# Scores two units ahead, one layer-1 buffer, and another ScalarE order in a hand-ordered cycle

## The chip, the cores and the metric

The kernel runs on one core of a Trainium2 chip. Its time is the device time of one launch, in microseconds (us), as the median of several runs. In the profile PE is TensorE (PEld its weight loads), DVE is VectorE, ACT is ScalarE, POOL is GpSimd, and SP is the engine that here only issues DMAs. A q behind an engine's name (ACTq, SPq) is its sequencer, for instance where it issues a DMA.

## What is computed

Three layers, all in fp32. The first is attention over 4 batches, 8 heads, 576 tokens and head size 64, in which each query keeps only its 32 largest scores. The other two are feed-forward layers over 2304 tokens, 512 wide with 2048 hidden channels: layer 1 with a rational function between its two products, layer 2 with h cos(h). Cut to what matters, the reference is:

```python
scores = scale * np.matmul(q, k.transpose(0, 1, 3, 2))
kth = np.partition(scores, -top_k, axis=-1)[..., -top_k:-top_k + 1]
scores = np.where(scores >= kth, scores, -1000000000.0)
attn = softmax(scores)
x = (attn @ v), heads side by side
h = x @ w_in1
P = a[0] + a[1] * h + a[2] * h**2 + a[3] * h**3
Q = 1.0 + np.abs(b[0]) * np.abs(h) + np.abs(b[1]) * h**2
x = (P / (Q + 1e-06)) @ w_out1
h = x @ w_in2
out = (h * np.cos(h)) @ w_out2
```

## The kernel before

**Units.** The work is cut into 72 attention units, numbered i: 128 queries for a pair of heads each. Eight units make one block of 256 tokens, and each of the feed-forward layers has eight groups (256 hidden channels) for a block. Group i-9 of layer 1 and group i-18 of layer 2 run beside unit i (UA = 9, UB = 18 line 39), so that each step of the outer loop holds a bit of all three layers. Units 64 to 71 are mixed: their queries come from two batches, so each loads two k tiles and two v tiles and has more, smaller matmuls.

**Attention.** `qk(i)` (line 313) makes the scores of a unit for two heads. TensorE multiplies q, split into a high and a low part, with k, four matmuls for each head, and ScalarE copies each head's scores out of PSUM into a tile sS (line 319, two buffers). `topk(i)` (line 341) runs on VectorE. It takes the elementwise max and min of the two halves of the scores (`tensor_tensor`), finds the 32nd largest by rounds of `max` and `match_replace` in a tile e, then ScalarE makes Exp into e, and in the last step, which is issued in the next unit, VectorE masks and sums (`scalar_tensor_tensor`). `av(i)` (line 390) transposes e on TensorE (pp), ScalarE copies the transposes (pt), and TensorE multiplies with v. q comes by DMA (`load_q`, line 179, tile qr); `high_q` (line 186) rounds it to the high part on ScalarE, and `low_q` subtracts. k comes by `load_k` (line 196, two buffers, shared by the two units of a pair), v by `load_v`. `prep` and `store_k` (lines 172 and 162) split the k of later batches and store both parts.

**Layer 1.** `in1` and `in1b` (two halves of h on TensorE), `copy1` (line 501: w = h and r = |h| on ScalarE), `lin1` (q and u on ScalarE), `pol1` (q and u multiplied on GpSimd), `rec1` (Ln and Exp into r on ScalarE), `mid1` and `end1` (lines 524 and 528: four passes on VectorE, then ScalarE copies the result's high part into gg), `low1` (its low part, GpSimd), `out1` (24 matmuls into y). The tiles w, q and r have N1 = 2 buffers, u has NU = 2.

**Layer 2.** `in2` and `in2b`, `phase2` (line 577: ScalarE copies h to hs, then makes rr and n from it), `mid2` (VectorE), `sin2` (one Sin on ScalarE over two groups, in even units: the sine units; it needs a table load), `table` (loads the table of Exp and Ln again), `mul2` (GpSimd), `high2` (ScalarE copies the high part into gg), `low2` (GpSimd), `out2` (12 matmuls into o). In each unit h of layer 1, h of layer 2 and the two pp share two PSUM buffers.

**Order.** Up to unit 19 and from step 72 on, a planner places the instructions (`free`, line 724, and `events`, line 774, give the order that it starts from). From unit 20 to 71 (U0 and U1), the fixed cycle, `unit(i, prev)` (line 806) writes the order out by hand: class `InOrder` ties each instruction of VectorE, ScalarE, GpSimd and TensorE to the one written before it on its engine. GpSimd's instructions also wait for the last VectorE instruction written before them that is not `max` or `match_replace`. DMAs of q, k and v are issued from ScalarE's queue, so they stand in its order too; weights come by SP, through four stream buffers. Four lines of `unit` carry most of what follows:

```python
            nq = qk(i + 1) if i + 1 < nu else iter(())
            ev(i - UB - 2, high2)
            ev(i - UB, phase2)
            high_q(i + 3)
```

`qk(i + 1)` stands between the halves of h, `high2` ahead of Exp, `phase2` and `high_q` at the end of ScalarE's unit, just ahead of the next unit's pt copies. What the diff touches, and what calls it:

Of the kernel before, what the change touches and what calls it, by code (L numbers as in the profile page):

```python
# [51 lines left out]
PM = 150  # L52
WA, PA = 12, 90
WG, PG = 10, 90
N1, NU, N2, NST, NGG = 2, 2, 2, 4, 3
SUBV = (3,)
CPE = (0, 2)
LAL = 3
DV1, DV2 = 8, 7
KB, VB, XB = 2, 2, 2  # L60
OBB, EB = 1, 2
QRB, QB = 2, 2
S0 = 46
U0, U1 = 20, 72
# [51 lines left out]
def body(tc, out, qt, kt, vt, ident_d, w1_d, w1o_d, a_d, b_d, w2_d, w2o_d):  # L116
# [5 lines left out]
    with ExitStack() as ctx:  # L122
# [60 lines left out]
                A.dma_start(out=raw, in_=qt[k, pr, :, :, i % 2 * P:(i % 2 + 1) * P])  # L183
                qs_[i] = [raw, None]

        def high_q(i):
            if 8 <= i < nu:
                qs_[i][1] = x = att.tile([P, 2, 2, P], F32R, tag="q", bufs=QB, name=f"q{i}")
                A.activation(x[:, 0], qs_[i][0], AF.Copy)

        def low_q(i, E):
            if 8 <= i < nu:
# [120 lines left out]
        def qk(i):  # L313
            n, pr = units[i]
            raw, x = qs_.pop(i)
            hi, lo = (x[:, 0], x[:, 1]) if x is not None else (None, None)
            kvs = ins[i]
            m = P // len(kvs)
            st[i] = sb = att.tile([P, 2, S], F32, tag="sS", bufs=2, name=f"sS{i}")
            for j in range(2):  # L320
                rows = slice(j * D, (j + 1) * D)
                for c, (k, _) in reversed(list(enumerate(kvs))):
                    qs = slice(0, (c + 1) * m)
                    for hf in range(2):
                        o = sx[qs, hf, :HALF]
                        hs = slice(hf * HALF, (hf + 1) * HALF)
                        if n < 2:
                            mm = PE.matmul(o, raw[rows, j, qs], k[rows, 0, hs].bitcast(F32), start=True, stop=True)
                            after(mm, hf)
                        else:  # L330
                            mm = PE.matmul(o, hi[:, j, qs], k[:, j, hs], start=True, stop=False, skip_group_check=True)
                            after(mm, hf)
                            mm = PE.matmul(o, lo[:, j, qs], k[:, j, hs], start=False, stop=True, skip_group_check=True)
                        order[hf] = [mm.ins.name]
                A.activation(halves(sb[:, j]), sx[:, :, :HALF], AF.Copy)
                if j == 0:
                    yield
            if n == 1:
                store_k(kvs[0][0], 0, pr)
# [234 lines left out]
        def in2b(k, g):  # L574
            g2[k, g][1](1)

        def phase2(k, g):
            h, _ = g2.pop((k, g))
            if g % SINB == 0:
                rp[k, g // SINB] = late[0].tile([P, SINB, 512], F32, tag="rr", bufs=2, name=f"rr{k}_{g}")  # L580
            rs = rp[k, g // SINB]
            rr = rs[:, g % SINB]
            hs = late[0].tile([P, 512], F32, tag="hs", bufs=N2, name=f"hs{k}_{g}")
            A.activation(hs, h, AF.Copy)
            n = late[0].tile([P, DM], F32, tag="n", bufs=OBB, name=f"n{k}_{g}")
            if k >= DV2:
                V.tensor_scalar(rr, hs, 1.0 / TWO_PI, 0.25, op0=ALU.mult, op1=ALU.add)
            else:
                A.activation(rr, hs, AF.Identity, scale=1.0 / TWO_PI, bias=quarter)
            A.activation(n, rr, AF.Identity, bias=magic)  # L590
            rt[k, g] = rr, hs, n
# [125 lines left out]
        preps = {}  # L717
        for b in range(1, B):
            for pr in range(NP):
                preps.setdefault(16 * b - PL + pr if b == 1 else 16 * b - PL + 1 + 2 * pr, []).append((b, pr))  # L720

        nrm, low, held, x2, ob = [], [], [], [], []

        def free(i, prev):
            nq = qk(i + 1) if i + 1 < nu else iter(())
            next(nq, None)
            next(nq, None)
            if i + 2 < nu:
                load_k(i + 2)
            t = topk(i) if i < nu else iter([None] * 9)  # L730
            fresh = []
            for p in range(5):
                if p == 0:
                    for x, a in held:
                        store_k(x, *a)
                    held[:] = [(prep(*a), a) for a in preps.get(i, [])]
                    if prev is not None:
                        next(prev)
                    next(t, None)
                    if prev is not None:  # L740
                        next(prev)
                    next(t, None)
                    if prev is not None:
                        a = av(i - 1)
                        next(a)
                        next(a, None)
                        if i % 4 == 0:
                            nrm.append(norm((i - 1) // 8, (i - 1) // 4 % 2))
                            next(nrm[-1])
                            next(nrm[-1])  # L750
                            fresh.append(nrm[-1])
                    if 0 < i < nu:
                        load_v(i)
                    low_q(i + 2, G)
                else:
                    next(t, None)
                if p == 1:
                    if i + 1 < 8:
                        load_q(i + 3)
                    if i + 2 >= 8:  # L760
                        load_q(i + 4)
                if p == 2:
                    high_q(i + 3)
                if fresh and p == 1:
                    next(fresh.pop())
                if len(nrm) == 2 and p in (1, 4):
                    for x in nrm[:1] if p == 1 else nrm[1:]:
                        next(x)
                        next(x, None)
                    if p == 4:  # L770
                        nrm.clear()
                yield t

        def events(u, p):
# [16 lines left out]
            if p == 2:  # L791
                if u < U0:
                    ev(u - UA - 1, end1, low1)
                ev(u - UB, in2, in2b, phase2)
            if p == 3:
                ev(u - UA - 1, out1)
                if last(u - UA - 1):
# [6 lines left out]
                    store((u - UB - 3) // NG, 1)  # L804

        def unit(i, prev):
            t = topk(i)
            next(t)
            next(prev)
            next(prev)  # L810
            a = av(i - 1)
            next(a)
            ev(i - UA - 1, mid1, end1)
            for x in low:
                next(x, None)
# [18 lines left out]
            ev(i - UB - 2, mul2)  # L834
            if i % 4 == 0:
                next(nrm[-1])
            ev(i - UA, in1b, copy1)
            nq = qk(i + 1) if i + 1 < nu else iter(())
            next(nq, None)
            ev(i - UA, lin1, pol1)  # L840
            ev(i - UB, in2)
# [2 lines left out]
            for k in ob:  # L844
                store(k, 1)
            ob.clear()
            if i + 2 < nu:
                load_k(i + 2)
            load_q(i + 4)
            load_v(i)  # L850
            ev(i - UA - 1, out1)
            ev(i - UB - 3, out2)
            ev(i - UB - 1, table)
            ev(i - UB - 2, high2)
            for _ in range(4):
                next(t)
            ev(i - UA, rec1)
            if i % 8 == 0:
                for x in nrm:
                    next(x)  # L860
                low.extend(nrm)
                nrm.clear()
            ev(i - UB, phase2)
            high_q(i + 3)
            if last(i - UA - 1):
                x2high((i - UA - 1) // NG)
                x2.append((i - UA - 1) // NG)
# [70 lines left out]
```

## Time and profile before

| | |
|---|---|
| three runs | 1452.74 us median (1451.27 to 1456.11) |
| the profiled execution's own time | 1454.12 us |
| its span, first to last instruction | 1452.3 us |
| busy in the span | PE 88%, PEld 77%, DVE 83%, ACT 76%, POOL 40% |
| mean granted TensorE clock | 0.922 |
| chain of work that ended last, by engine | PE 45%, ACT 20%, DMA 3%, issue 3%, DVE 2% |

The busy shares are means over stages that differ: a head with weight conversion and a cold clock, the fixed cycle, and a tail without attention. A unit of the fixed cycle is told by VectorE's max/min pair (`e<-sS`, TENSOR_TENSOR), which starts it; the pair of unit 22 starts at 402.3 us, that of unit 64 at 1109.6. The granted clock is a share of 2.4 GHz: 1.00 is that level, 0.5 is 1.2 GHz, and what lies between is a stretch with some of each. Almost all instructions are recorded under one helper's line (L80), so groups go by the tiles' names, out<-in.

### The profile page before, as it was taken

How to read it: one execution, taken by the hardware profiler on the slowest of the kernel's cores; microseconds unless marked ns; L12 is line 12 of the kernel's file. 1: busy time of each engine (PE TensorE's matmuls, PEld its weight loads, DVE VectorE, ACT ScalarE, POOL GpSimd, SP SyncE). 2: the span in 40 equal slices, each digit the busy share in tenths (PEclk: the TensorE clock that was granted, in tenths of full speed). 3: DMA queues.
4: the chain of work that ended last, by engine and by line, in shares of the span. 5: the costliest groups of instructions: out<-in, count | busy, mean ns of one | idle time of the engine just before them, and what ended most of it. 6: DMA issues, size and time to landing. Idle time of an engine off the chain costs nothing.

```text
span 1452.3 us, 25010 instructions
## 1 busy us (share of the span) xinstructions
PE 1272.2 (88%) x8944; PEld 1121.2 (77%) x8944; DVE 1200.8 (83%) x2514; ACT 1100.5 (76%) x1918; POOL 585.1 (40%) x434
## 2 busy tenths in 40 slices
PE   6777776667799999999998999999999899999988
PEld 3434555556788888888888888888888788899976
DVE  7989997898888988889899889989998778755532
ACT  7777887866688887878888778878887667777642
POOL 3666455633344444444444443534444324430000
PEclk9567797878899999999999999999999999999999
DMA  8986777862366676556677755655666667667667
GB/s 267 333 273 208 222 228 252 292 202 80 102 204 206 214 230 212 190 178 207 211 227 232 235 185 186 198 197 192 207 206 228 239 224 258 216 207 247 227 217 233
DMA packets 155948, 314.98 MB, mean 217 GB/s; under 512 B 12592, under 2 KB 47536, under 8 KB 155824
## 3 DMA queue, kind: packets, MB, share of 16 engines
q1 hardware_dynamic: 122832, 261.99, 54.4%
q10 hardware_dynamic: 32992, 51.39, 11.1%
q8 instruction: 71, 1.16, 0.3%
q14 instruction: 53, 0.43, 0.1%
HBM read 278.20 MB, written 35.13 MB: 216 GB/s over the span
## 4 chain that ended last, share of the span: by engine, by line
PE 45%; ACT 20%; DMA 3%; issue 3%; DVE 2%; ACTq 2%; POOL 1%; SPq 0%
PE h L80 22%; PE sx L80 9%; PE y L80 7%; PE o L80 6%; ACT r L80 4%; ACT e L80 3%; ACTq L80 2%; ACT q L80 2%; ACT rr L80 2%; DMA lo<-w2lo 1%; ACT n L80 1%; ACT gg L80 1%; DMA w2o<-w2o 1%; ACT sS L80 1%; DVE e L80 1%
## 5 line engine op out<-in xcount | busy, mean ns | idle before, releaser
L80 DVE MAX8 hd<-e 128x8 f32<-128x288 f32 (+1 forms) x576 | 320.7, 596 | 0.0
L80 DVE TENSOR_TENSOR e<-sS 128x576 f32<-128x576 f32 x144 | 172.9, 1240 | 87.1 <-ACT sS L80 74.2
L80 PE MATMUL y<-gg,w1o 128*128 128x256 f32 x1152 | 219.7, 289 | 13.3 <-DVE x2l L80 6.5
L80 DVE MATCH_REPLACE8 e<-hd,e 128x288 f32<-128x288 f32 (+1 forms) x432 | 231.0, 541 | 0.0
L80 PE MATMUL h<-xh,w1hi 128*128 128x256 f32 x576 | 183.2, 318 | 47.9 <-ACT pt24a L80 2.1
L80 PE MATMUL o<-w2o,gg 128*128 128x512 f32 x864 | 212.1, 393 | 3.6 <-DMA w2o<-w2o 3.5
L80 POOL TENSOR_TENSOR gg<-rr,gg 128x512 fp32r<-128x512 f32 x56 | 72.5, 1295 | 315.6 <-DVE rr L80 84.1
L80 PEld LDWEIGHTS y<-gg,w1o 128*128 128x128 f32 x1152 | 184.9, 196 | 16.6 <-ACT gg L80 11.5
L80 PEld LDWEIGHTS o<-w2o,gg 128*128 128x128 f32 x864 | 157.5, 189 | 35.0 <-DMA w2o<-w2o 4.7
L80 PE MATMUL h<-xh,lo 128*128 128x256 f32 x576 | 171.4, 298 | 0.9 <-DMA lo<-w1lo 0.9
L80 PE MATMUL h<-xl,w1hi 128*128 128x256 f32 x576 | 170.9, 297 | 0.0
L80 PEld LDWEIGHTS h<-xh,w1hi 128*128 128x128 f32 x576 | 117.7, 204 | 68.8 <-issue 7.1
L80 PE MATMUL h<-x2h,lo 128*128 128x256 f32 x576 | 164.0, 285 | 3.0 <-DMA lo<-w2lo 3.0
L80 PE MATMUL y<-gg,w1ol 128*128 128x256 f32 x576 | 165.3, 287 | 0.0
L80 PE MATMUL h<-x2h,w2hi 128*128 128x256 f32 x576 | 163.5, 284 | 0.5 <-ACT hs L80 0.5
L80 PE MATMUL h<-x2l,w2hi 128*128 128x256 f32 x576 | 163.6, 284 | 0.1
L80 DVE SCALAR_TENSOR_TENSOR e<-sS,hd,e 128x576 f32<-128x576 f32 x144 | 123.1, 883 | 39.3 <-ACT e L80 39.3
L80 POOL TENSOR_TENSOR q<-q,r 128x512 f32<-128x512 f32 x64 | 86.2, 1347 | 133.3 <-ACT q L80 133.3
L80 POOL TENSOR_TENSOR cb<-cb,raw 128x512 int32<-128x512 int32 x64 | 92.8, 1454 | 73.2 <-DVE cb L80 59.6
L80 PEld LDWEIGHTS h<-xh,lo 128*128 128x128 f32 x576 | 118.5, 206 | 1.4 <-DMA lo<-w1lo 1.4
L80 PEld LDWEIGHTS h<-xl,w1hi 128*128 128x128 f32 x576 | 118.4, 206 | 1.0 <-issue 0.7
L80 PE MATMUL sx<-k,q 128*128 128x288 f32 (+1 forms) x576 | 106.8, 313 | 11.2 <-ACT xs L80 9.1
(1023 smaller groups left out, 3343.0 us busy)
## 6 DMA issues: line engine op xcount, KB each, us to landing
w2o<-w2o SPq DMA_DIRECT2D x144, 512.0 KB, 4.4
lo<-w1lo SPq DMA_DIRECT2D x72, 512.0 KB, 4.6
w1ol<-w1ol SPq DMA_DIRECT2D x72, 512.0 KB, 4.9
lo<-w2lo SPq DMA_DIRECT2D x72, 512.0 KB, 4.2
k<-kdr ACTq DMA_DIRECT2D x44, 576.0 KB, 3.9
raw<-w SPq DMA_DIRECT2D x32, 512.0 KB, 4.9
v<-vt ACTq DMA_DIRECT2D x48, 320.0 KB, 6.2
qr<-qt ACTq DMA_DIRECT2D x72, 128.0 KB, 3.9
```

The lines of the kernel that those rows point to most:

```text
L80: r = f(*a, **k)
```

## The change

The scores of unit i+2, not i+1, are made in unit i of the fixed cycle; sS gets a third buffer, an extra `qk` at the end of unit 19 starts the lead, and `load_k` and `prep` shift by one unit with it. w, q and r of layer 1 get one buffer instead of two. q's high part is a GpSimd copy within the cycle, between `mul2` and `pol1`. `phase2` is cut in two: `copy2` (hs) stays in its unit, the rest runs at the end of units without the sine, and early in the next unit for a group whose own unit has the sine. `high2` moves behind `rec1` and `copy2`, `load_q` up behind `copy1`, `load_v` down behind Exp.

```diff
@@ -52,13 +52,13 @@
 PM = 150
 WA, PA = 12, 90
 WG, PG = 10, 90
-N1, NU, N2, NST, NGG = 2, 2, 2, 4, 3
+N1, NU, N2, NST, NGG = 1, 2, 2, 4, 3
 SUBV = (3,)
 CPE = (0, 2)
 LAL = 3
 DV1, DV2 = 8, 7
 KB, VB, XB = 2, 2, 2
-OBB, EB = 1, 2
+OBB, EB, SB = 1, 2, 3
 QRB, QB = 2, 2
 S0 = 46
 U0, U1 = 20, 72
@@ -183,10 +183,13 @@
                 A.dma_start(out=raw, in_=qt[k, pr, :, :, i % 2 * P:(i % 2 + 1) * P])
                 qs_[i] = [raw, None]
 
-        def high_q(i):
+        def high_q(i, grouped=False):
             if 8 <= i < nu:
                 qs_[i][1] = x = att.tile([P, 2, 2, P], F32R, tag="q", bufs=QB, name=f"q{i}")
-                A.activation(x[:, 0], qs_[i][0], AF.Copy)
+                if grouped:
+                    G.tensor_copy(x[:, 0], qs_[i][0])
+                else:
+                    A.activation(x[:, 0], qs_[i][0], AF.Copy)
 
         def low_q(i, E):
             if 8 <= i < nu:
@@ -316,7 +319,7 @@
             hi, lo = (x[:, 0], x[:, 1]) if x is not None else (None, None)
             kvs = ins[i]
             m = P // len(kvs)
-            st[i] = sb = att.tile([P, 2, S], F32, tag="sS", bufs=2, name=f"sS{i}")
+            st[i] = sb = att.tile([P, 2, S], F32, tag="sS", bufs=SB, name=f"sS{i}")
             for j in range(2):
                 rows = slice(j * D, (j + 1) * D)
                 for c, (k, _) in reversed(list(enumerate(kvs))):
@@ -574,14 +577,17 @@
         def in2b(k, g):
             g2[k, g][1](1)
 
+        def copy2(k, g):
+            h, _ = g2.pop((k, g))
+            hs = late[0].tile([P, 512], F32, tag="hs", bufs=N2, name=f"hs{k}_{g}")
+            A.activation(hs, h, AF.Copy)
+            rt[k, g] = hs
+
         def phase2(k, g):
-            h, _ = g2.pop((k, g))
+            hs = rt[k, g]
             if g % SINB == 0:
                 rp[k, g // SINB] = late[0].tile([P, SINB, 512], F32, tag="rr", bufs=2, name=f"rr{k}_{g}")
-            rs = rp[k, g // SINB]
-            rr = rs[:, g % SINB]
-            hs = late[0].tile([P, 512], F32, tag="hs", bufs=N2, name=f"hs{k}_{g}")
-            A.activation(hs, h, AF.Copy)
+            rr = rp[k, g // SINB][:, g % SINB]
             n = late[0].tile([P, DM], F32, tag="n", bufs=OBB, name=f"n{k}_{g}")
             if k >= DV2:
                 V.tensor_scalar(rr, hs, 1.0 / TWO_PI, 0.25, op0=ALU.mult, op1=ALU.add)
@@ -717,7 +723,7 @@
         preps = {}
         for b in range(1, B):
             for pr in range(NP):
-                preps.setdefault(16 * b - PL + pr if b == 1 else 16 * b - PL + 1 + 2 * pr, []).append((b, pr))
+                preps.setdefault(16 * b - PL + pr if b == 1 else 16 * b - PL + 2 + 2 * pr, []).append((b, pr))
 
         nrm, low, held, x2, ob = [], [], [], [], []
 
@@ -769,6 +775,10 @@
                         next(x, None)
                     if p == 4:
                         nrm.clear()
+                if i == U0 - 1 and p == 4:
+                    for _ in qk(i + 2):
+                        pass
+                    load_k(i + 3)
                 yield t
 
         def events(u, p):
@@ -791,7 +801,7 @@
             if p == 2:
                 if u < U0:
                     ev(u - UA - 1, end1, low1)
-                ev(u - UB, in2, in2b, phase2)
+                ev(u - UB, in2, in2b, copy2, phase2)
             if p == 3:
                 ev(u - UA - 1, out1)
                 if last(u - UA - 1):
@@ -804,12 +814,15 @@
                     store((u - UB - 3) // NG, 1)
 
         def unit(i, prev):
+            sine = (i - UB - 1) % SINB == SINB - 1
             t = topk(i)
             next(t)
             next(prev)
             next(prev)
             a = av(i - 1)
             next(a)
+            if not sine:
+                ev(i - UB - 1, phase2)
             ev(i - UA - 1, mid1, end1)
             for x in low:
                 next(x, None)
@@ -834,8 +847,10 @@
             ev(i - UB - 2, mul2)
             if i % 4 == 0:
                 next(nrm[-1])
+            high_q(i + 3, True)
             ev(i - UA, in1b, copy1)
-            nq = qk(i + 1) if i + 1 < nu else iter(())
+            load_q(i + 4)
+            nq = qk(i + 2) if i + 2 < nu else iter(())
             next(nq, None)
             ev(i - UA, lin1, pol1)
             ev(i - UB, in2)
@@ -844,24 +859,24 @@
             for k in ob:
                 store(k, 1)
             ob.clear()
-            if i + 2 < nu:
-                load_k(i + 2)
-            load_q(i + 4)
-            load_v(i)
+            if i + 3 < nu:
+                load_k(i + 3)
             ev(i - UA - 1, out1)
             ev(i - UB - 3, out2)
             ev(i - UB - 1, table)
-            ev(i - UB - 2, high2)
             for _ in range(4):
                 next(t)
+            load_v(i)
             ev(i - UA, rec1)
             if i % 8 == 0:
                 for x in nrm:
                     next(x)
                 low.extend(nrm)
                 nrm.clear()
-            ev(i - UB, phase2)
-            high_q(i + 3)
+            ev(i - UB, copy2)
+            ev(i - UB - 2, high2)
+            if not sine or i == U1 - 1:
+                ev(i - UB, phase2)
             if last(i - UA - 1):
                 x2high((i - UA - 1) // NG)
                 x2.append((i - UA - 1) // NG)
```

## Rows read from the trace of the kernel before

**Rows 1.** Stages: us, busy of PE, PEld, DVE, ACT, POOL; PEclk, DMA share, GB/s

```profile
0.00:362.60 362.60, 257.43 (x1303) 187.97 (x1303) 319.25 (x657) 269.85 (x512) 185.90 (x140) 0.78 0.73 236
362.60:402.30 39.70, 31.95 (x235) 29.60 (x236) 31.00 (x67) 26.44 (x48) 14.62 (x11) 0.83 0.33 106
402.30:1109.60 707.30, 665.60 (x5045) 611.45 (x5044) 638.26 (x1384) 577.75 (x1003) 313.49 (x230) 0.97 0.63 207
1109.60:1262.00 152.40, 140.48 (x1164) 130.63 (x1164) 120.34 (x265) 111.87 (x191) 54.77 (x44) 0.97 0.67 235
1262.00:1452.30 190.30, 176.71 (x1204) 161.53 (x1202) 91.94 (x144) 114.57 (x167) 16.36 (x13) 0.98 0.69 227
```

**Rows 2.** The same view for units 35, 38 and 40

```profile
623.67:642.33 18.66, 16.43 (x118) 15.00 (x117) 14.69 (x33) 12.62 (x23) 5.89 (x5) 0.91 0.54 195
...
675.08:690.51 15.43, 15.29 (x121) 14.09 (x120) 14.82 (x32) 13.99 (x24) 6.94 (x6) 1.00 0.61 198
...
707.07:722.92 15.85, 15.71 (x125) 14.51 (x124) 15.06 (x35) 14.53 (x25) 8.19 (x7) 1.00 0.55 177
```

**Rows 3.** Waits, 402 to 1110 us: total us, times, longest

```profile
POOL q L80 <- ACT q L80: 105.6, 43, 5.0
...
DVE e L80 <- ACT sS L80: 47.4, 38, 2.9
...
DVE e L80 <- ACT e L80: 22.3, 21, 2.0
```

**Rows 4.** The chain that ended last, 600 to 760 us: start, us, what

```profile
632.62 2.93 PE h L80 x12
...
673.95 1.43 PE h L80 x12
...
681.01 0.45 PE pp37a L80 x4
...
703.26 0.54 PE sx L80 x4
```

**Rows 5.** PE's timeline: start, us, instruction, [idle before, what ended it]

```profile
632.62 0.58 PE L80 MATMUL h<-xh,w1hi 128*128 128x256 f32 x1 [1.53 <-ACT pt34a L80]
```

**Rows 6.** ACT's timeline, 689 to 708 us

```profile
689.85 0.63 ACT L80 ACTIVATE sS<-sx 128x576 f32<-128x576 f32 x1
...
691.07 1.28 ACT L80 ACT_TABLE_LOAD   x1 [0.59 <-issue]
...
693.12 1.45 ACT L80 ACTIVATE e<-sS,nb 128x576 f32<-128x576 f32 x2
...
696.37 0.72 ACT L80 ACTIVATE rr<-hs,quarter 128x512 f32<-128x512 f32 x1
...
697.75 0.40 ACT L80 ACTIVATE q<-qr 128x256 fp32r<-128x256 f32 x1
698.05 0.58 ACT L80 ACTIVATE pt38a<-pp38a 128x512 f32<-128x512 f32 x1
...
706.40 0.64 ACT L80 ACTIVATE sS<-sx 128x576 f32<-128x576 f32 x1
...
707.69 1.45 ACT L80 ACTIVATE e<-sS,nb 128x576 f32<-128x576 f32 x2
```

**Rows 7.** POOL's groups, 402 to 1110 us: busy us, mean ns | idle before

```profile
L80 POOL TENSOR_TENSOR u<-u,w 128x512 f32<-128x512 f32 x43 | 76.5, 1780 | 0.0
...
L80 POOL TENSOR_TENSOR gg<-rr,gg 128x512 fp32r<-128x512 f32 x42 | 54.0, 1285 | 231.0 <-DVE rr L80 61.3 <-DVE x2l L80 35.3 <-ACT pt56t L80 8.7
```

**Rows 8.** The tile e on DVE, whole span: ns min/median/max, first and last start

```profile
L80 DVE TENSOR_TENSOR e<-sS x144: 734/945/1965, 10.9 to 1245.1; 128x576 f32<-128x576 f32 x144
```

**Rows 9.** DVE's timeline, q's low part in unit 39

```profile
698.18 0.43 DVE L80 TENSOR_TENSOR q<-qr,q 128x256 fp32r<-128x256 f32 x1
```

**Rows 10.** Timelines of ACT, then DVE, at the edge of unit 20

```profile
360.57 0.80 ACT L80 ACTIVATE q<-r,babs 128x512 f32<-128x512 f32 x1
...
361.63 1.02 DVE L80 SCALAR_TENSOR_TENSOR u<-q,u 128x512 f32<-128x512 f32 x1
```

## The prediction

> **What bounds the kernel now.** I read the stages first. The fixed cycle (units 20 to 71) has three pieces: two starting units, 42 plain units from 402.3 to 1109.6 us, and eight mixed units to about 1262 [rows 1]. The 42 take 707.3 us, 16.84 us each. No engine is busy that long: TensorE 665.6 us (15.85 a unit), VectorE 638.3 (15.20), ScalarE 577.8 (13.76). TensorE's mean granted clock is 0.97, so some of its 665.6 us ran at 1.2 instead of 2.4 GHz; taking 0.03 x 707.3 = 21.2 us off leaves 644.4, or 15.34 us a unit.
>
> Single units come next. One in which nothing stalls takes 15.43 us at a clock of 1.00; one in four that also transposes the softmax sums takes 15.85; an odd one took 18.66 at 0.91 [rows 2]. So 3/4 x 15.43 + 1/4 x 15.85 = 15.54 us is what TensorE needs, and 1.30 us a unit is lost, mostly in the odd units. The waits tell on what: VectorE waits 47.4 us in these 42 units for the copy of scores (sS) and 22.3 us for Exp (e) [rows 3]. TensorE's loss shows in the chain of waits: twelve matmuls of h from 632.62 took 2.93 us [rows 4], after 1.53 us of idling for ScalarE's copy of the transposes (pt34a) [rows 5].
>
> ScalarE's timeline says why the copy was late. The second score copy (sS) of unit 38 starts at 689.85. DMA issues keep the table load until 691.07, Exp starts at 693.12, phase2's rr at 696.37, the q copy at 697.75, and pt38a only at 698.05: 8.20 us. In the next unit the piece from sS to Exp is 707.69 - 706.40 = 1.29 us, and with the same 4.93 us behind Exp that makes 6.22 [rows 6]. TensorE in the meantime has its last half of h, y and o, and the next transposes: from 673.95 to 681.01 + 0.45 = 7.51 us [rows 4]. So after one unit of two ScalarE is late by 0.7 us even if Exp never waits for VectorE, and it does wait, because VectorE only gets the scores that were made within the same unit.
>
> **The change part by part.**
> *Scores two ahead, three sS buffers.* The eight score matmuls and two copies a unit stay where they are on their engines; only their index moves. The max/min of the next unit then finds its scores a unit old. The 47.4 us of waits go [rows 3], and VectorE may run ahead. What is late next for VectorE is Exp. A new wait: qk(i+2) now needs low_q(i+2) of the same unit. VectorE made q's low part at 698.18 [rows 9] and the scores' matmuls came at 703.26 [rows 4]: 5.1 us of cover, costed at nothing; without it up to that much would go onto TensorE, with y and o queued behind. load_k runs a unit earlier and keeps its two buffers and its one-unit lead; its issue moves from sine units, where the table load waits for it, to the others. prep and its stores on SP move a unit later with it, off the unit of the k load, so no two of them fight for a buffer: nothing.
>
> *ScalarE's order.* In a sine unit the stretch from sS to pt loses the DMA issues in front of the table load (691.07 less 689.85 + 0.54 of sS = 0.68), the q copy (0.30) and rr and n of phase2 (697.75 - 696.37 = 1.38): 8.20 - 2.36 = 5.84 us. In the other it loses only q: 6.22 - 0.30 = 5.92 [rows 6]. high2's copy moves behind Exp inside that stretch and weighs the same. Both are below TensorE's 7.51 by 1.6 us, which is what VectorE may keep Exp waiting. The deferred phase2 (1.38) goes where ScalarE waits for TensorE in the next unit, which has no sine; VectorE's mid2 waits for it, at most that long, and max and match_replace queue behind; the new lead covers it. load_q is issued under the copies of w and r, load_v under Exp: nothing, if their buffers are free, as they are by a unit.
>
> *One buffer for w, q and r.* copy1 must then wait for end1 of the group before. VectorE is through with end1 when it starts q's low part (698.18) [rows 9], before the scores' matmuls (703.26) [rows 4] that follow the half of h that copy1 reads: covered. In the whole trace the second buffer is used once, at the edge of the cycle: ScalarE writes the new q at 360.57 while VectorE reads the old one until 361.63 + 1.02 = 362.65 [rows 10]. That costs 2.1 us at most; I take it whole.
>
> *q by GpSimd.* No row has a one-input copy on GpSimd. The nearest, a two-input pass over 128x512, is 1.285 us, so half of it for 256 columns, 0.64, and the dearest row, u at 1.78, bound it [rows 7]; I take 0.64, the row of the same engine without contention, scaled. GpSimd idles 105.6 us before the q product, 2.5 a unit [rows 3]: hidden at either end. Below nothing it cannot go; what ScalarE gains is counted above. In the Trainium skill, the page "GPSIMD Engine Reference", section "Engine selection", speaks against elementwise work on GpSimd but calls one-input passes roughly line-rate. No run here shows that; by it the sum stays and the slower rival below would have no chance.
>
> *The sum.* TensorE needs 15.54 us a plain unit; VectorE, if it keeps today's 22.3 / 42 = 0.53 of Exp waits, needs 15.20 + 0.53 = 15.73. I take 15.85, a little above both, for the joints between engines that no longer have slack: 42 x (16.84 - 15.85) = 41.6 us. The bounds are 15.54 (54.6) and 16.84 (0). The mixed units take 152.4 / 8 = 19.05; TensorE's need is 140.5 less 0.03 x 152.4, over 8, or 17.0 [rows 1]. I take 17.6, since each loads two k and two v and k keeps its place in ScalarE's queue: 8 x 1.45 = 11.6, between 0 and 16.4. The first two units take 39.7 with VectorE busy 31.0 [rows 1]; scores made ahead in unit 19 save about half of the 8.7: 4.3, between 0 and 8.7. Less 2.1. Together 41.6 + 11.6 + 4.3 - 2.1 = 55.4. The head (362.6 us) and the tail (190.3, TensorE busy 176.7) [rows 1] keep their order of work; I put them at 0, within 5 us either way, since they are placed by a planner that sees other buffers. The profiled execution took 1454.1 us (its span and 1.8 around it): 1398.7. It is 1.4 us above the median of the runs, so 1397.
>
> **The rivals.** *ScalarE still holds TensorE.* VectorE has only 1.6 us of ScalarE's margin. If Exp comes later than that in units without the sine, where two phases stand behind it, the transposes' copy is late in every second unit, TensorE idles and its clock falls. In rows, the same twelve matmuls cost 2.93 us after idling [rows 4], and the unit ran at 0.91 [rows 2]. For it: all three engines then need 14 to 15.7 us of 15.9. Against: VectorE's lead outlasts the late phase2. With a third of today's 1.30 recovered the plain units give 18, the mixed 6, the rest 0: about 1430. The Trainium skill, "TensorE: Matmul & The Clock Gate", section "What's actually happening", has the clock throttled by default and released by activity. The trace agrees (0.91 after idling, 1.00 without), and by that rule what is left of the stalls would keep paying double.
>
> *VectorE's max/min keeps colliding with GpSimd.* A max/min pass takes 0.73 us at least and 0.945 in the median [rows 8]; u on GpSimd, which runs beside it, takes 1.78 where the same shape takes 1.285 [rows 7]. The 15.20 holds this already, so with it VectorE is at 15.73, inside the forecast.
>
> *Slower: the copy on GpSimd.* It stands before both products of pol1, and Ln waits for q. The cover is 2.5 us a unit [rows 3]; past that each us of copy is a us of unit, and the gain of 0.99 is gone at about 3.5, plus what ScalarE's margin takes, 1.6: from some 5 us the kernel is slower. A copy of 7 would cost 2 us x 50 units: about 1550. Against: it would be four times the dearest row.
>
> *The scores come no earlier in effect.* If the k tiles, still two, made qk(i+2) wait, VectorE would get its scores as now and only ScalarE's order would help: some 10 us, 1443. Against: k is needed a unit earlier and is loaded a unit earlier.
>
> **How the numbers follow.** Forecast 0.74; ScalarE holds TensorE 0.14; scores no earlier 0.05, half of it within what can't be told from no change; GpSimd or something like it slower 0.05; no effect 0.02. A measurement of this kernel tells 0.3%, 4.4 us, from no change. Faster 0.74 + 0.14 + 0.025 rounds to 0.91, same 0.04, slower 0.05. The low end has every bound of the sum at its best but for the last us of each: 54.6 + 16.4 + 8.7 - 2.1 = 77.6, or 1375; the high end reaches past the first rival, 1432.
>
> **What would show it.** Right: plain units of 15.5 to 16.2 us in place of 15.4 and 16.5 to 19; VectorE's waits for sS gone, those for Exp left; granted clock 1.00 over the 42 units; table loads without DMA issues in front; the GpSimd copy near 0.6 us. Wrong: TensorE idle before h for pt copies in every second unit; qk waiting for q's low part or for q from GpSimd; ScalarE's w waiting for VectorE; head or tail longer by over 5 us.

## The result, and the profile after

The changed kernel takes 1387.89 us in the median of four runs (1384.79 to 1389.19), against 1452.26 for the kernel before measured with it: a ratio of 0.9549, with a 95% interval of 0.9525 to 0.9573. The profiled execution took 1387.8 us, with a span of 1386.0. The forecast was 1397, in a range of 1375 to 1432.

The stages of the span, with the columns of [rows 1], cut at the starts of units 20, 22 and 64 and behind unit 71:

```profile
0.00:361.40 361.40, 242.68 (x1290) 179.53 (x1291) 321.56 (x656) 269.03 (x512) 181.06 (x138) 0.82 0.73 237
361.40:396.10 34.70, 31.78 (x268) 29.18 (x268) 30.86 (x66) 28.61 (x50) 19.50 (x15) 1.00 0.41 134
396.10:1061.20 665.10, 652.70 (x5051) 598.65 (x5050) 625.80 (x1386) 566.82 (x962) 312.52 (x271) 1.00 0.67 221
1061.20:1194.00 132.80, 130.03 (x1119) 121.02 (x1118) 111.99 (x261) 105.73 (x178) 55.89 (x47) 1.00 0.73 254
1194.00:1386.00 192.00, 178.88 (x1225) 164.16 (x1224) 96.28 (x149) 116.72 (x172) 19.15 (x15) 0.98 0.69 228
```

The plain stretch fell from 707.3 to 665.1 us: 15.84 us a unit, with TensorE busy 652.7 of it (15.54 a unit) at a clock of 1.00. TensorE's busy time fell by 12.9 us and its idle time by 29.3. The 42 units give back 42.2 us, the starting units 5.0, units 64 to 70 17.2 (19.15 to 16.69 us a unit, by the starts of units 64 and 71: 1109.60 and 1243.65 before, 1061.17 and 1177.99 after), and head and tail together 1.8. That is the 66.3 us by which the span is shorter.

Units now come in unequal pairs, because VectorE runs ahead in one and waits in the next; a pair is the right measure. The same view for units 36 and 37, then 38 and 39:

```profile
618.00:649.67 31.67, 31.17 (x245) 28.62 (x244) 29.45 (x68) 27.58 (x48) 15.19 (x14) 1.00 0.64 216
649.67:680.94 31.27, 30.80 (x241) 28.26 (x240) 29.07 (x66) 25.59 (x44) 13.93 (x13) 1.00 0.66 212
```

The waits from 396 to 1061 us, which answer to [rows 3]:

```profile
DVE rr L80 <- ACT n L80: 37.2, 21, 2.4
POOL q L80 <- ACT q L80: 33.2, 39, 2.3
...
PEld sx L80 <- ACT sS L80: 12.6, 40, 0.6
```

VectorE's groups, with the idle time before them at the end of the line:

```profile
L80 DVE TENSOR_TENSOR e<-sS 128x576 f32<-128x576 f32 x85 | 90.0, 1098 | 0.0
L80 DVE SCALAR_TENSOR_TENSOR e<-sS,hd,e 128x576 f32<-128x576 f32 x84 | 65.0, 809 | 0.3 <-ACT e L80 0.3
```

VectorE's 47.4 us for sS are gone, and of the 22.3 for Exp 0.3 is left. In their place VectorE waits in every second unit for n of the deferred phase2, 1.8 us in the mean; none of TensorE's idle time is put down to that wait. TensorE's groups by what idled before them say where its time was lost. The line of h is the kernel's before, then that of the changed kernel, each in its own fence, with busy time, mean ns, and idle time before the group:

```profile
L80 PE MATMUL h<-xh,w1hi 128*128 128x256 f32 x336 | 106.8, 318 | 36.9 <-ACT pt24a L80 2.1 <-ACT pt40a L80 2.1 <-ACT pt42a L80 1.9
```

```profile
L80 PE MATMUL h<-xh,w1hi 128*128 128x256 f32 x336 | 103.4, 308 | 7.9 <-ACT pt25a L80 1.0 <-ACT pt41a L80 1.0 <-ACT pt57a L80 0.4
...
L80 PE MATMUL sx<-k,q 128*128 128x288 f32 (+1 forms) x352 | 65.1, 309 | 4.5 <-ACT sS L80 1.4
```

TensorE idled 36.9 us before h in the kernel before, nearly all of it for ScalarE's copies of the transposes, and 7.9 after; this is the number to follow through the experiments. Of the 7.9, 5.2 are 0.14 us in each of 37 units, which is there even where ScalarE itself waits for TensorE; 2.7 us, in units 25, 33, 41, 49 and 57, lie behind a late copy. The second line is a small new wait: 4.5 us ahead of the score matmuls.

ScalarE's timeline over a sine unit (36), to be held against [rows 6]:

```profile
629.49 0.63 ACT L80 ACTIVATE r<-w 128x512 f32<-128x512 f32 x1
629.50 0.56 ACTq L80 DMA_DIRECT2D qr<-qt  x1
630.11 0.65 ACT L80 ACTIVATE sS<-sx 128x576 f32<-128x576 f32 x1
...
632.07 0.63 ACT L80 ACTIVATE sS<-sx 128x576 f32<-128x576 f32 x1
632.72 1.28 ACT L80 ACT_TABLE_LOAD   x1
...
634.25 0.78 ACT L80 ACTIVATE e<-sS,nb 128x576 f32<-128x576 f32 x1
...
637.36 0.62 ACT L80 ACTIVATE gg<-rr 128x512 fp32r<-128x512 f32 x1
639.15 0.60 ACT L80 ACTIVATE pt36a<-pp36a 128x512 f32<-128x512 f32 x1 [1.17 <-PE pp36a L80]
```

From the second sS to the end of the last copy it is 637.98 - 632.07 = 5.91 us, where 8.20 stood before and 5.84 was forecast, and then ScalarE waits 1.17 us for TensorE. The roles are turned round. From the second sS to the start of the pt copy it is 639.15 - 632.07 = 7.08 us; this is the time that TensorE leaves ScalarE, which the prediction had put at 7.51.

### The profile page after: what moved, and what is told of

Same layout as the page of the kernel before. It is cut to its first block, busy times and chain, and to the rows that moved or that the text cites. A ratio compares the mean times of both kernels' runs of the same rounds, so it can differ in the third digit from the quotient of the medians.

```text
span 1386.0 us, 25042 instructions
## 1 busy us (share of the span) xinstructions
PE 1236.1 (89%) x8944; PEld 1092.5 (79%) x8944; DVE 1186.5 (86%) x2514; ACT 1086.9 (78%) x1869; POOL 588.1 (42%) x483
## 4 chain that ended last, share of the span: by engine, by line
PE 51%; ACT 17%; DVE 15%; DMA 10%; issue 3%; POOL 2%; SPq 0%; ACTq 0%; POOLq 0%; DVEq 0%
PE h L80 19%; PE o L80 11%; PE y L80 10%; PE sx L80 8%; DVE e L80 7%; DVE hd L80 5%; ACT r L80 2%; ACT sS L80 2%; DMA lo<-w1lo 2%; DMA w2o<-w2o 2%; ACT e L80 1%; ACT rr L80 1%; ACT n L80 1%; DMA w2lo<-cb 1%; POOL cb L80 1%
## 5 line engine op out<-in xcount | busy, mean ns | idle before, releaser
L80 PE MATMUL y<-gg,w1o 128*128 128x256 f32 x1152 | 216.9, 287 | 9.9 <-POOL gg L80 6.9
L80 PE MATMUL h<-xh,w1hi 128*128 128x256 f32 x576 | 179.4, 312 | 11.1 <-ACT pt13a L80 1.4
L80 PE MATMUL h<-xh,lo 128*128 128x256 f32 x576 | 167.9, 291 | 1.6 <-DMA lo<-w1lo 1.6
L80 DVE TENSOR_TENSOR e<-sS 128x576 f32<-128x576 f32 x144 | 148.7, 1070 | 7.7 <-ACT sS L80 5.1
L80 DVE SCALAR_TENSOR_TENSOR e<-sS,hd,e 128x576 f32<-128x576 f32 x144 | 127.7, 914 | 15.6 <-ACT e L80 15.6
L80 ACT ACTIVATE e<-sS,nb 128x576 f32<-128x576 f32 x144 | 105.7, 770 | 19.6 <-DVE hd L80 18.5
L80 PEld LDWEIGHTS h<-xh,lo 128*128 128x128 f32 x576 | 114.7, 199 | 2.5 <-DMA lo<-w1lo 2.2
L80 PEld LDWEIGHTS h<-xl,w1hi 128*128 128x128 f32 x576 | 115.0, 200 | 2.1 <-DVE xl L80 1.2
```

The source lines that it names most:

```text
L80: r = f(*a, **k)
```

## The experiments

Two theories. Theory A, the prediction's emphasis: VectorE waited for scores, so the lead of two units is what counts. Theory B: ScalarE's copies came late and stopped TensorE; the new order is what counts, and the lead little. The table holds the whole study. A plain unit is 1/42 of the time from the start of unit 22 to that of unit 64, a mixed one 1/7 of that from 64 to 71, and the last column is the idle time of TensorE before h in the plain units, as in the fences above; these three are of one profiled execution each. That of phase_whole took 1400.1 us, 5 above its median, that of phase_loads 1401.2, 4 below.

| kernel | median us | plain unit | mixed unit | idle before h |
|---|---|---|---|---|
| before | 1452.3 | 16.84 | 19.15 | 36.9 |
| one_buffer | 1448.2 | 16.87 | 18.83 | 37.1 |
| lead_only | 1420.3 | 16.31 | 18.80 | 28.1 |
| no_lead (order only) | 1395.1 | 15.91 | 17.63 | 6.6 |
| no_lead_phase | 1401.2 | 16.06 | 17.48 | 17.5 |
| phase_loads | 1405.3 | 16.01 | 17.82 | 20.1 |
| phase_whole | 1395.4 | 15.97 | 17.06 | 13.0 |
| q_scalar | 1392.0 | 15.93 | 17.02 | 11.5 |
| high2_old | 1388.9 | 15.84 | 16.71 | 5.9 |
| loads_old | 1387.0 | 15.74 | 17.33 | 8.7 |
| changed | 1387.9 | 15.83 | 16.69 | 7.9 |
| q_five | 1400.4 | 16.13 | 16.84 | 6.3 |
| loadq_later | 1385.6 | 15.74 | 16.91 | 9.2 |
| loadq_split | 1384.4 | 15.75 | 17.01 | 9.1 |

The medians carry some 2 to 4 us either way. The head of the profiled executions, up to unit 20, ranged from 358.4 to 363.9 us among kernels that differ from the changed one only within unit(), so differences of a few us between totals are not read; the units are steadier.

### The lead and the order apart

Without the lead:

```diff
-            nq = qk(i + 2) if i + 2 < nu else iter(())
+            nq = qk(i + 1) if i + 1 < nu else iter(())
-            if i + 3 < nu:
-                load_k(i + 3)
+            if i + 2 < nu:
+                load_k(i + 2)
```

(and the extra qk at the end of unit 19 out, prep a unit earlier).

> The changed kernel with the scores of unit i+1 again made in unit i (k load and prep back with them); ScalarE's order, the one buffer and the GpSimd copy stay. Theory A (the lead is what counts, since VectorE waited for scores): VectorE waits for sS again, some 1 us a unit in the fixed cycle, and the time is 1430 to 1445. Theory B (ScalarE's late copies held TensorE, the lead only helps at the edges): within 12 us of the changed kernel, below 1400.

And the kernel before with the lead alone (with the extra qk at the end of unit 19, prep a unit later, N1 = 1 and three sS buffers, as in the changed kernel):

```diff
-            nq = qk(i + 1) if i + 1 < nu else iter(())
+            nq = qk(i + 2) if i + 2 < nu else iter(())
-            if i + 2 < nu:
-                load_k(i + 2)
+            if i + 3 < nu:
+                load_k(i + 3)
```

> The kernel before with the scores two ahead, three sS buffers, one buffer for w, q, r, and the k load and prep that go with them; ScalarE's order and its q copy stay as before. Theory A: only the sine units stay late, by ScalarE's 8.20 against TensorE's 7.51 us, 0.7 us in two units or 15.9 us a unit: 1395 to 1410, with VectorE's waits for sS gone. Theory B: ScalarE's late copies still stop TensorE and its clock falls: 1430 to 1450, granted clock below 0.99 in the plain units.

Measured: 1395.14 us without the lead (ratio 0.959, 0.9564 to 0.9616), 1420.3 with the lead alone (0.9776, 0.9752 to 0.98). Theory A fails on the first; the second lies between the two forecasts. The run without the lead brings 57 of the 64 us: the order, with q's copy on GpSimd and the one buffer, which is worth 4 us by itself (below). TensorE before h, and then VectorE's wait for scores among the waits of the plain units, in the run without the lead:

```profile
L80 PE MATMUL h<-xh,w1hi 128*128 128x256 f32 x336 | 103.5, 308 | 6.6 <-ACT pt40a L80 0.5 <-ACT pt24a L80 0.5
```

```profile
DVE e L80 <- ACT sS L80: 4.6, 14, 1.3
```

VectorE's wait for scores went from 47.4 to 4.6 us although the scores are made in the same unit as before. So that wait was a symptom. The traces fit the reading that scores came late because TensorE had stood still for the transposes' copies: in the kernels without the lead TensorE's idle time before h and VectorE's wait for scores fall together, 36.9 and 47.4 us, 17.5 and 12.3 (no_lead_phase), 6.6 and 4.6. In the first of them the clock was 0.97 besides, in the other two 1.00. With the lead alone, VectorE does not wait for scores at all, but TensorE's line and the plain stretch read:

```profile
L80 PE MATMUL h<-xh,w1hi 128*128 128x256 f32 x336 | 103.8, 309 | 28.1 <-ACT pt32a L80 1.5 <-ACT pt48a L80 1.5 <-ACT pt24a L80 1.5
```

```profile
395.30:1080.20 684.90, 655.71 (x5069) 601.49 (x5068) 659.60 (x1385) 581.79 (x1008) 310.17 (x229) 1.00 0.64 216
```

The clock is at 1.00 here too, so theory B's forecast of a clock under 0.99 missed, and so did its time, which this run undercuts by 10 us; the copies are still late. Nor does this run leave ScalarE's work in the sine units as it was: the issue of k's load, and in eight of them prep's copy of k (0.67 us), move to the other units with the lead. The two parts overlap. In a plain unit, the lead is worth 16.87 - 16.31 = 0.56 us with the old order (against one_buffer) and 15.91 - 15.83 = 0.08 with the new; the order 0.96 without the lead and 0.48 with it. In a mixed unit they do more together than apart: from one_buffer's 18.83, the lead alone brings 0.03 us, the order alone 1.20, both 2.14. Some 0.4 of what the lead brings there is only moved: with it the seven units hold 96 to 100 score matmuls, without it 112, because the scores of one mixed unit are made earlier.

### One buffer

```diff
-N1, NU, N2, NST, NGG = 2, 2, 2, 4, 3
+N1, NU, N2, NST, NGG = 1, 2, 2, 4, 3
```

> The kernel before with one buffer for w, q and r and nothing else. By the prediction it costs at most 2.1 us at the edge of unit 20 and otherwise only what the planner makes of it in the head: 1447 to 1459. Rival: in the head copy1 holds TensorE's PSUM buffer while it waits for end1, and the head grows by 10 us or more.

Measured: 1448.23 us, ratio 0.9973 (0.9956 to 0.999). Within the range, on the good side: units 20 and 21 took 33.8 us instead of 39.7, the head 366.3 instead of 362.6. The planner placed the work around the edge differently; the 2.1 us did not show as a loss. The plain units did not change (16.87).

### The order, part by part

Each of these undoes one part of ScalarE's order in the changed kernel. phase2 whole:

```diff
-            if not sine:
-                ev(i - UB - 1, phase2)
-            if not sine or i == U1 - 1:
-                ev(i - UB, phase2)
+            ev(i - UB, phase2)
```

> The changed kernel with rr and n of phase2 again at the end of every unit's ScalarE work; nothing is deferred. Theory M (a margin: each part of the new order matters only once the parts together pass TensorE's 7.51 us): a sine unit's stretch from sS to pt grows from 5.84 to 7.22 us, still below 7.51, and VectorE no longer waits for the deferred n: plain units 15.8 to 15.95 us, the time 1384 to 1396. Theory P (each part pays its own us, since Exp waits for VectorE and the margin is used up): 1.38 us in two units, 0.7 a unit: 1415 to 1425.

load_q and load_v behind load_k again:

```diff
-            load_q(i + 4)
             nq = qk(i + 2) if i + 2 < nu else iter(())
...
             if i + 3 < nu:
                 load_k(i + 3)
+            load_q(i + 4)
+            load_v(i)
...
-            load_v(i)
             ev(i - UA, rec1)
```

> The changed kernel with load_q and load_v again behind load_k, ahead of the table load and Exp. Theory M: a sine unit's stretch grows by 0.6 us to 6.5, below 7.51, and the first score copy is no longer delayed by load_q: plain units 15.7 to 15.85 us; the mixed units, which issue two k, q and two v there, get 1 us longer each: 1388 to 1396. Theory P: 0.3 us a unit and 1.5 in the mixed: 1408 to 1418.

high2 ahead of Exp again:

```diff
             ev(i - UB - 1, table)
+            ev(i - UB - 2, high2)
...
             ev(i - UB, copy2)
-            ev(i - UB - 2, high2)
```

> The changed kernel with high2's copy again ahead of Exp. The stretch from sS to pt keeps its length; Exp is 0.54 us later. Theory M: VectorE waits about 2 us in every second unit for n anyway and can take that: within 4 us of 1388. Theory P (Exp sets VectorE's pace): 0.5 us a unit: 1408 to 1416.

q rounded by ScalarE at the end of the unit:

```diff
-            high_q(i + 3, True)
...
             if not sine or i == U1 - 1:
                 ev(i - UB, phase2)
+            high_q(i + 3)
```

> The changed kernel with q rounded by ScalarE again, behind phase2 at the end of the unit (0.30 us there). Theory M: within 4 us of 1388. Theory P: 0.3 us a unit where the copies are late: 1400 to 1406.

Measured, in this order: 1395.39 (ratio 0.96, 0.9576 to 0.9625), 1387.0 (0.9538, 0.9518 to 0.9558), 1388.89 (0.9549, 0.952 to 0.9577) and 1391.99 us (0.9573, 0.9556 to 0.9589). All four lie far below theory P and at theory M's forecasts, or within 1 us of them: loads_old came out 1 us below its range, and phase_whole's plain unit of 15.97 just above its 15.95. In a plain unit the four undone parts cost 0.14, -0.09, 0.01 and 0.10 us, 0.16 together, and yet all four undone, which is lead_only, cost 0.48. Undone alone, a part mostly hides in the margin that the others leave; the units below show how. The exception are the loads in the mixed units: 17.33 against 16.69 us.

Two at once, the diffs of phase2 whole and of the loads together:

> The changed kernel with two parts undone at once: phase2 whole in every unit, load_q and load_v behind load_k; the lead, the GpSimd copy and high2's place stay. Alone they cost 7 us and nothing. Theory M (a margin that the parts share): a sine unit's stretch from sS to pt is 5.84 + 1.38 + 0.68 = 7.9 us, past TensorE's 7.51, so together they cost more than the sum: plain units 16.15 to 16.35 us, the time 1405 to 1418. Additive: plain units 15.85 to 16.0, and with the mixed units' DMA issues 1392 to 1400.

Measured: 1405.33 us (0.967, 0.9644 to 0.9695). More than the sum of the two (about 1394), as theory M has it. In the units the excess is smaller than it said: the plain ones took 16.01, where the sum gives 15.88 and the forecast was 16.15 to 16.35, and the mixed ones 17.82, which is little above the sum of 17.70. TensorE before h, with phase2 whole alone and then with both:

```profile
L80 PE MATMUL h<-xh,w1hi 128*128 128x256 f32 x336 | 103.3, 307 | 13.0 <-ACT pt40a L80 1.3 <-ACT pt56a L80 1.3 <-ACT pt32a L80 1.3
```

```profile
L80 PE MATMUL h<-xh,w1hi 128*128 128x256 f32 x336 | 103.3, 307 | 20.1 <-ACT pt56a L80 1.5 <-ACT pt40a L80 1.5 <-ACT pt24a L80 1.5
```

The idle time climbs 7.9, 13.0, 20.1, 28.1 (lead_only) as parts are put back; it does not jump at 7.51 us. Unit by unit there is a limit nearby. Of the 21 sine units, five (24, 32, 40, 48 and 56) hold two more copies of ScalarE (xh, about 1.05 us). The table has the median of ScalarE's stretch, from the start of the second sS to the end of its last pass before the pt copy, and of TensorE's idle time before h behind it, in us:

| kernel | 16 sine units: stretch | idle | 5 with xh: stretch | idle |
|---|---|---|---|---|
| changed | 5.91 | 0.14 | 6.95 | 0.14 |
| loads_old | 6.08 | 0.14 | 7.13 | 0.14 |
| q_scalar | 6.22 | 0.14 | 7.26 | 0.20 |
| phase_whole | 7.28 | 0.22 | 8.32 | 1.26 |
| phase_loads | 7.45 | 0.39 | 8.54 | 1.47 |
| lead_only | 7.90 | 0.85 | 8.93 | 1.53 |
| one_buffer | 8.89 | 1.53 | 9.94 | 1.53 |

Up to 7.13 us the idle time is the 0.14 named above; from 7.26 to 8.54 it grows by a us with each us of the stretch, whichever part was put back. The limit between 7.13 and 7.26 is the 7.08 us from sS to the pt copy: a pass right behind another starts some 0.1 us before that one ends (677.26 below, for 676.63 + 0.72). So theory M's mechanism holds, with a cover of 7.08 us, not 7.51: phase_whole alone passes it in nearly every sine unit, the other parts only in units with more copies. (Above 8.9 the idle time before h stays at 1.5; where the rest goes was not followed.) Unit 38 of phase_whole, ScalarE and then TensorE; the pt copy starts 677.26 - 670.08 = 7.18 us after the second sS:

```profile
670.08 0.63 ACT L80 ACTIVATE sS<-sx 128x576 f32<-128x576 f32 x1
...
676.63 0.72 ACT L80 ACTIVATE n<-rr,magic 128x512 f32<-128x512 f32 x1
677.26 0.57 ACT L80 ACTIVATE pt38a<-pp38a 128x512 f32<-128x512 f32 x1
```

```profile
677.89 0.39 PE L80 MATMUL h<-xh,w1hi 128*128 128x256 f32 x1 [0.21 <-ACT pt38a L80]
```

And phase2 whole in the kernel without the lead (its diff and that of the run without the lead together):

> The run without the lead, and phase2 whole as well. If the lead is worth little because the order's margin covers what it would cover (theory M), then with the margin spent the lead is worth more than the 7 us that it is worth in the changed kernel: against the run with phase2 whole and the lead (1395) this one is 15 to 30 us slower, 1410 to 1425, and VectorE waits for sS again. If the lead is worth about 7 us whatever the order: 1400 to 1405.

Measured: 1401.21 us (0.9646, 0.9622 to 0.9669), 6 us over phase_whole. This one went against theory M: with phase2 whole the lead is worth no more than with it split. VectorE waited 12.3 us for sS. The table above names one thing that the lead does for the old order: from one_buffer to lead_only the stretch shortens by 1.0 us, and the load and the copy of k leave the sine units. How much of the 0.56 us a unit that explains was not taken apart.

### The GpSimd copy

```diff
-                    G.tensor_copy(x[:, 0], qs_[i][0])
+                    for _ in range(5):
+                        G.tensor_copy(x[:, 0], qs_[i][0])
```

> The changed kernel with q's high part copied five times over by GpSimd: 1.6 us more in front of pol1's products. It measures the cover that the slower rival was priced with. By the trace of before (2.5 us a unit) it hides: within 4 us of 1388. By the trace of the changed kernel GpSimd idles only 33.2 us before the q product, 0.8 a unit: the other 0.8 us reaches Ln, and with two products later beside max/min also VectorE: 1395 to 1430.

Measured: 1400.42 us (0.9642, 0.9615 to 0.9668). GpSimd's groups over the plain units, first of the changed kernel, then of this run:

```profile
L80 POOL TENSOR_TENSOR u<-u,w 128x512 f32<-128x512 f32 x43 | 62.0, 1441 | 0.0
...
L80 POOL CAST q<-qr 128x256 fp32r<-128x256 f32 x42 | 16.8, 399 | 0.0
```

```profile
L80 POOL CAST q<-qr 128x256 fp32r<-128x256 f32 x210 | 84.6, 403 | 10.6
L80 POOL TENSOR_TENSOR u<-u,w 128x512 f32<-128x512 f32 x42 | 76.3, 1816 | 0.0
L80 POOL TENSOR_TENSOR q<-q,r 128x512 f32<-128x512 f32 x43 | 60.9, 1416 | 0.0
```

And the plain stretch of this run, with the columns of [rows 1]:

```profile
396.70:1073.90 677.20, 654.43 (x5050) 598.56 (x5050) 658.70 (x1385) 568.77 (x962) 397.62 (x439) 1.00 0.66 217
```

One copy takes 0.40 us, and 1.6 us more of it cost 0.3 us in each plain unit. So 1.6 us did not hide, and the 2.5 us of [rows 3] was not the cover: in the changed kernel GpSimd's wait for ScalarE's q is down from 105.6 to 33.2 us, and the copy accounts for only 16.8 of the difference. The expectation named two routes for the loss, Ln and VectorE. VectorE's is seen: its busy time rose from 625.8 to 658.7 us. How the 0.3 us divide between the two was not taken apart, so the run gives no clean figure for the cover.

### load_q once more

```diff
-            load_q(i + 4)
             nq = qk(i + 2) if i + 2 < nu else iter(())
             next(nq, None)
             ev(i - UA, lin1, pol1)
+            load_q(i + 4)
```

> The changed kernel with load_q behind lin1 instead of between copy1 and the first score copy. In the changed kernel the first score copy starts when r ends (0.62 us after r's start, against 0.53 in the kernel before) and TensorE's second scores come just behind it. If the issue of the DMA costs that, each unit shortens by 0.1 to 0.2 us and the time falls by 5 to 10 us, to 1378 to 1383. If the second scores are held by something else: within 2 us of 1388.

Measured: 1385.62 us (0.9533, 0.9517 to 0.955). The wait that it aimed at went:

```profile
L80 PE MATMUL sx<-k,q 128*128 128x288 f32 (+1 forms) x352 | 64.9, 308 | 0.5 <-ACT sS L80 0.3
```

The plain unit fell by 0.09 us, just short of what was expected; the total by 2.3, which the intervals cannot tell from nothing.

A last run takes that edit for the plain units alone:

```diff
-            load_q(i + 4)
+            if i >= 61:
+                load_q(i + 4)
             nq = qk(i + 2) if i + 2 < nu else iter(())
             next(nq, None)
             ev(i - UA, lin1, pol1)
+            if i < 61:
+                load_q(i + 4)
```

> The changed kernel with load_q behind lin1 up to unit 60 and behind copy1 from there. With load_q behind lin1 throughout, TensorE's 4.5 us of idling before score matmuls in the plain units went (15.83 to 15.74 us a unit), and the mixed units took 16.9 us against 16.7. If both are of the order, not chance, this takes the better half of each: 3 to 6 us below the changed kernel, 1382 to 1385. Otherwise as the run before: 1385 to 1388.

Measured: 1384.38 us (0.9537, 0.9514 to 0.956), the lowest median and still not clear of the changed kernel. Its mixed units, whose load_q stands where the changed kernel has it, took 17.01 us, so the 0.2 us that this run meant to win back was not of load_q's place.

## Why the prediction was right, and where not

The time lay 9 us below the forecast, within the range. By its steps:

- *TensorE's need, 15.54 us a plain unit.* Measured busy time: 652.7 / 42 = 15.54, clock 1.00. The forecast unit of 15.85 came as 15.83, and 41.6 us of gain as 42.2. The other bound, VectorE's 15.73 us, was none: VectorE was busy 625.8 / 42 = 14.90 us a unit and waited 0.3 us in all for Exp, where the prediction expected those waits to stay.
- *ScalarE's order.* 8.20 to 5.84 us forecast in a sine unit, 5.91 measured, and the late copies nearly gone (36.9 to 7.9 us). Right in mechanism. The lateness itself was put too low: 8.20 is unit 38's, among the shorter ones, the median from sS to pt is 8.79 (9.84 with xh), and the cover is 7.08, not 7.51, so TensorE stood still 1.5 us in a sine unit rather than 0.7.
- *The lead.* This step failed. "The 47.4 us of waits go" was booked under it, but the waits go with ScalarE's order alone (4.6 us left), and the rival "the scores come no earlier in effect", priced at 1443, is nearly the run without the lead: 1395. The prediction had found that ScalarE is late by 0.7 us in every second unit and did not follow it on: TensorE's idling and VectorE's late scores went with that lateness; the clock came back with either part. The sum stood because it went by each engine's need and not by what each part brings.
- *The mixed units.* Sized at 17.6 us, measured 16.69: 0.91 a unit, 6.4 us over seven. TensorE's need, put at 17.0, was nearly right for the same work: in no_lead_phase, whose window holds as many matmuls as before, it is busy 117.78 / 7 = 16.83 us at a clock of 1.00. The changed kernel has less in the window, 114.19 / 7 = 16.31 us: the lead has moved one unit's scores ahead of it, and, cut as it is at VectorE's starts, it holds 11 fewer matmuls of layer 2's h. So part of the gain there is work moved, which the prediction did not price. That k keeps its place in ScalarE's queue was said to hold the units up; moving q and v out of its way was worth 0.64 us a unit (loads_old). TensorE's score matmuls over the seven units, before and then after:

```profile
L80 PE MATMUL sx<-k,q 128*128 128x288 f32 x56 | 9.8, 297 | 0.0
L80 PE MATMUL sx<-k,q 128*64 128x288 f32 x56 | 9.6, 294 | 0.0
```

```profile
L80 PE MATMUL sx<-k,q 128*128 128x288 f32 x48 | 8.4, 297 | 0.0
L80 PE MATMUL sx<-k,q 128*64 128x288 f32 x48 | 8.2, 294 | 0.0
```

- *The starting units.* 5.0 us for 4.3 looks right and was luck. The 4.3 was booked under the lead, with the one buffer as a loss of 2.1 there. But units 20 and 21 fell from 39.7 to 33.8 us in one_buffer and to 32.8 without the lead; with lead and one buffer (lead_only) they took 34.4.
- *Small terms.* The one buffer's 2.1 us not seen; head and tail 1.8 for 0. mid2 does wait for the deferred phase2, 1.8 us in the mean rather than 1.38 at most, under VectorE's lead, as said.
- *ScalarE still holds TensorE*, the likeliest rival: 2.7 us of late copies are left, in five of the 42 units.
- *The slower rival.* Its price was wrong. It counted 2.5 us of cover and 1.6 of margin; q_five shows a loss of 12.5 us for 1.6 us of copy. The copy itself came cheaper than taken, 0.40 us for 0.64. The Trainium skill's "GPSIMD Engine Reference", section "Engine selection", calls one-input passes roughly line-rate. The trace agrees in direction, 0.40 us for 256 columns where half of a two-input pass over 512 is 0.64; how near to line-rate that is no run here shows.

The fall of the clock was sized at 21.2 us, 0.03 of the plain stretch. The clock did come back to 1.00, with either part of the change, but TensorE's busy time fell by 12.9 us only (665.6 to 652.7). The forecast's 15.54 us a unit was read from single units at 1.00 and does not rest on that figure.

## What to carry to other kernels

The engine with the longest wait need not be where the time is lost: here VectorE's 47 us for scores went when ScalarE's order was changed and nothing was done for the scores. When several small moves of a fixed order are proposed, compare the late engine's stretch with the cover of the engine that waits for it, kind of unit by kind of unit, and read the cover where the engine is not late (7.08 us here); undone one by one the moves look worthless (0.16 us a unit) while together they are worth three times that. A cover read from idle time before an edit holds only for the pace before it.

## What the runs showed of the hardware

A DMA issue between two ScalarE passes costs their overlap: sS starts 0.62 us after r with load_q's issue in between (629.49, 630.11 above), and 0.54 after it in the kernel before, where no issue lies between. Over the 42 plain units it is 0.61 to 0.69 in the changed kernel, and 0.54 in the kernel before and in loadq_later. From the kernel before:

```profile
639.18 0.63 ACT L80 ACTIVATE r<-w 128x512 f32<-128x512 f32 x1
639.72 0.63 ACT L80 ACTIVATE sS<-sx 128x576 f32<-128x576 f32 x1
```

VectorE's max/min pair depends on its neighbour, as two lines of its timeline in the changed kernel show, of units 37 and 38:

```profile
631.92 3.29 DVE L80 TENSOR_TENSOR e<-sS 128x576 f32<-128x576 f32 x2
...
649.67 1.41 DVE L80 TENSOR_TENSOR e<-sS 128x576 f32<-128x576 f32 x2
```

The first runs beside both of pol1's products on GpSimd (631.54 to 634.60), the second as they end (649.77). The difference of 1.88 us is covered here: later in unit 37 VectorE waits 2.11 us for n. And the head, planned from nearly the same work, took between 358.4 and 366.3 us over these kernels, more than several of the parts under test.
